# A two-stage kernel on one core: the first two chunks reordered, the softmax front one batch sooner, the sums in two tiles, the last batch step-major

## The chip, the core and the metric

The kernel runs on one core of one Trainium2 chip. The time is that of one execution on the device, in microseconds, from the first instruction to the last write of the output. Several executions are timed, and one more is taken by the hardware profiler. Five engines work side by side and wait for each other through semaphores: TensorE (PE, with PEld for its weight loads), VectorE (DVE), ScalarE (ACT), GpSimd (POOL) and SyncE (SP), which here issues all DMAs. Each engine takes its instructions in the order in which the program wrote them.

## The reference

A dynamic convolution over 7 taps with weights from a softmax, followed by a feed-forward layer with a squared ReLU. `x` is 8 x 4096 x 192 (32768 tokens), the weights of the convolution are one row of 7 for each token and each of 8 heads, and the matrices `w_in` (192 x 2048) and `w_out` (2048 x 192) come as float64.

```python
w = exp(weight_gen - max(weight_gen, -1))
w = w / (sum(w, -1) + 1e-09)
out = einsum('bshk,bskhg->bshg', w, x_unf)   # x_unf: the 7 tokens up to each, by head
h = out.reshape(B * S, D) @ w_in
g = maximum(h, 0) ** 2
return g @ w_out
```

## The kernel before

The 32768 tokens are cut into 64 chunks of 512 (four tiles of 128 tokens, `TC`). A chunk passes three stages: the convolution (`conv_steps`, on DVE, exponential on ACT), which leaves 192 x 512 numbers with the features on the partitions; the first matmul (`mm1`) with `w_in`, 2048 features in 8 groups `j` of 256; ReLU and square on ACT; and the second matmul (`mm2`) with `w_out` into the sums `acc` in PSUM, one tile of four banks.

From chunk 1 on both matmuls work in float16 pairs: a number is a high part and a low part. `xh`/`xl` are those of x, `gh`/`gl` those of g, `W` holds two parts of `w_in`, `V` three columns of `w_out` (hi, lo, and hi shifted down, "sh"). Chunk 0 is computed in float32, since the scales of the pairs are not known yet: the float64 weights are decoded meanwhile (`dec(u, step)`: unit u of 8, four of `w_in` and four of `w_out`, steps 0 on ACT, 1 on POOL (unit 0: DVE), 2 to 4 on DVE, 5 the largest magnitude), and then converted (`cvt[u]`: hi on ACT, lo on DVE, and sh on ACT for `w_out`).

The main loop at L581 runs over chunks c and batches b = 0 to 3, two groups j each. In a batch the program writes: `mm1` of both groups; `gl` of the batch before ("late"); at b = 1 the end of the chunk before (`finish`: `tmp` on ACT and `o_sb` on DVE for each half of acc, then `store`); at b = 3 the split of the next chunk's x; `mm2` of the batch before; then ACT's six activations (relu, square, relu, high, square, high), and last what stands in the table `todo` for this (c, b). `plan_conv(m)` deals the steps of chunk m's convolution onto that table. The first matmul of a batch fills two tiles `ph`, of which there are two, so relu must have read one before the next group can use it.

The convolution ends in a turn from tokens to features. Chunks below `N_PE` turn on PE by matmuls with the identity (L328), into the two `ph` tiles; the others by a DVE transpose of 32 x 32 blocks and a DMA to DRAM (`xd`) and back (`xT`). The split reads `xT` or `ph`: a cast on ACT (`xh`), then a subtract on DVE (`xl`).

The steps of one convolution, in order: maximum, subtract, exponential (ACT), sum, reciprocal, norm, seven products (mul) with six sums (add) between them, turn. Inputs come in groups of two chunks (`load_group`), with a scale for each group (`size_steps`: `total` on ACT, `scales` on DVE).

Of the kernel before, what the change touches and what calls it, by code (L numbers as in the profile page):

```python
# [25 lines left out]
def kernel(  # L26
# [366 lines left out]

    def mm2_first(fb):
        if fb == 0:
            accs[0] = ps_o.tile([P, TC, N], F32, name="acc")
        j, i = divmod(fb, 2)
        v = wfull[NU + j // 2][:, j % 2, i * D:(i + 1) * D]
        for t in range(TC):
            o = accs[0][:, t, 0:D]  # L400
            nc.tensor.matmul(o, rgs[0, j][:, i, t * P:(t + 1) * P], v, start=fb == 0, stop=fb == NF - 1)  # L401

    def mm2(c, b):
        if b == 0:
            accs[c] = ps_o.tile([P, TC, N], F32, name="acc")
        acc = accs[c]
        for t in range(TC):
            for j in (2 * b, 2 * b + 1):
                for i in range(2):
                    fb = 2 * j + i  # L410
                    first, last = fb == 0, fb == NF - 1
                    two = [(ghs[c, j], 0, 2 * D, 0), (gls[c, j], 0, D, 2 * D)]
                    if last:
                        two.reverse()
                    for n, (g, c0, c1, v0) in enumerate(two):
                        nc.tensor.matmul(  # L416
                            acc[:, t, c0:c1], g[:, i, t * P:(t + 1) * P], V[:, fb, v0:v0 + c1 - c0],
                            start=first and n == 0, stop=last and n == 1,
                        )
        for j in (2 * b, 2 * b + 1):  # L420
# [17 lines left out]
    def store(c):  # L438
        nc.sync.dma_start(out=out_v[:, c * TC:(c + 1) * TC, :], in_=outs.pop(c))
# [217 lines left out]
```

## Time and profile before

| | us |
|---|---|
| three runs, median (lowest to highest) | 2166.41 (2163.73 to 2166.71) |
| profiled execution | 2165.77 |
| its span, first to last instruction | 2164.0 |
| busy: PE, DVE, ACT, POOL | 2099.1, 1735.5, 1760.0, 9.1 |
| mean granted clock of PE | 0.995 |

The profile lists instructions with their start, duration and tiles; in square brackets the idle time of the engine before it and what ended that. Busy PE is near its whole span, but matmuls overlap in the records, so the distances between starts say more than busy time. "L416" is a line of the kernel before.

### The profile page before, as it was taken

What the parts mean: (1) busy time and instruction counts of PE and PEld (TensorE: products, weight loads), DVE (VectorE), ACT (ScalarE), POOL (GpSimd) and SP (SyncE); (2) the same over time, 40 slices, a digit from 0 to 9 for tenths busy, and PEclk for the clock granted to TensorE, in tenths of its full rate; (3) what the DMA queues carried; (4) which work ended last, traced back from release to release, by engine and by line L of the source; (5) the groups of instructions that cost most, each with busy time, mean ns of one, the idle gap of its engine ahead of it and who ended that gap; (6) DMA issues with size and microseconds to landing.
All of it is one profiled execution on the core that took longest, in us unless ns stands there. A gap on an engine that the chain in (4) does not pass through costs nothing.

```text
span 2164.0 us, 41491 instructions
## 1 busy us (share of the span) xinstructions
PE 2099.1 (97%) x17652; PEld 1182.8 (55%) x17652; DVE 1735.5 (80%) x2302; ACT 1760.0 (81%) x2006; POOL 9.1 (0%) x14
## 2 busy tenths in 40 slices
PE   7789999999999999999999999999999999999998
PEld 5555555555555555555555555555555555555555
DVE  7668878878878878878878878878878878778773
ACT  5667888888888888888888888888888888888886
POOL 1000000000000000000000000000000000000000
PEclk9999999999999999999999999999999999999999
DMA  6111222231222221222221232231232231232220
GB/s 176 38 38 47 73 89 78 71 89 44 75 89 74 76 89 38 81 89 69 80 89 38 82 89 67 82 89 38 82 89 67 82 89 37 83 89 66 54 60 15
DMA packets 99466, 156.26 MB, mean 72 GB/s; under 512 B 8281, under 2 KB 63705, under 8 KB 95313
## 3 DMA queue, kind: packets, MB, share of 16 engines
q1 hardware_dynamic: 99280, 153.61, 24.0%
q8 instruction: 138, 2.26, 0.4%
q14 instruction: 48, 0.39, 0.1%
HBM read 104.82 MB, written 48.76 MB: 71 GB/s over the span
## 4 chain that ended last, share of the span: by engine, by line
PE 78%; DVE 10%; ACT 9%; issue 2%; DMA 0%; SPq 0%; ACTq 0%
PE acc L416 40%; PE ph L373 36%; DVE gl L392 6%; ACT g L384 3%; ACT g L380 3%; ACT gh L388 1%; PE acc L401 1%; ACT tmp L435 1%; DVE o_sb L436 1%; DVE sm L264 1%; DVE sm L263 1%; ACT wt L262 1%; DVE pr L281 0%; PE ph L328 0%; DVE pr L276 0%
## 5 line engine op out<-in xcount | busy, mean ns | idle before, releaser
L416 PE MATMUL acc<-V,gh 128*128 128x384 f16 x4032 | 1024.1, 328 | 19.1 <-DVE o_sb L436 12.7
L416 PE MATMUL acc<-V,gl 128*128 128x192 f16 x4032 | 950.4, 247 | 16.1 <-DVE gl L392 16.1
L373 PE MATMUL ph<-xh,W 64*128 64x512 f16 x6048 | 778.9, 377 | 3.7 <-DVE xl L310 3.7
L373 PEld LDWEIGHTS <-W 64*128 64x128 f16 x9072 | 422.0, 94 | 540.4 <-issue 63.0
L380 ACT ACTIVATE g<-ph 128x1024 f32<-128x1024 f32 x504 | 510.3, 1013 | 209.8 <-PE ph L373 209.8
L392 DVE SCALAR_TENSOR_TENSOR gl<-gh,g 128x1024 f16<-128x1024 f16 x504 | 591.9, 1214 | 37.0 <-ACT gh L388 37.0
L416 PEld LDWEIGHTS <-gh 128*128 128x128 f16 x4032 | 392.0, 98 | 335.6 <-issue 84.2
L384 ACT ACTIVATE g<-g 128x1024 f32<-128x1024 f32 x512 | 538.2, 1052 | 8.0
L388 ACT ACTIVATE gh<-g 128x1024 f16<-128x1024 f32 x504 | 530.1, 1052 | 8.0
L416 PEld LDWEIGHTS <-gl 128*128 128x128 f16 x4032 | 395.1, 98 | 64.6 <-DVE gl L392 35.9
L276 DVE TENSOR_TENSOR pr<-xt,wt 128x768 f32<-128x768 f32 x448 | 416.2, 952 | 1.3 <-DMA xt<-in_x_dram 1.2
L373 PE MATMUL ph<-xl,W 64*128 64x512 f16 x3024 | 408.8, 376 | 0.0
L281 DVE TENSOR_TENSOR pr<-pr 128x768 f32<-128x768 f32 x382 | 363.7, 952 | 2.3
L263 DVE TENSOR_REDUCE sm<-wt 128x32 f32<-128x224 f32 x64 | 24.7, 386 | 285.1 <-ACT wt L262 285.1
L435 ACT ACTIVATE tmp<-acc,f 128x384 f32<-128x384 f32 x126 | 73.1, 580 | 123.6 <-DVE o_sb L436 117.9
L436 DVE SCALAR_TENSOR_TENSOR o_sb<-acc,f,tmp 128x384 f32<-128x384 f32 x126 | 77.4, 614 | 45.0 <-ACT tmp L435 45.0
L310 DVE TENSOR_TENSOR xl<-xT,xh 128x512 f16<-128x512 f32 x180 | 113.3, 684 | 0.0
L309 ACT CAST xh<-xT 128x512 f16<-128x512 f32 x180 | 98.5, 610 | 0.0
L344 DVE STREAM_TRANSPOSE xr<-pr 128x768 f32<-128x768 f32 x60 | 58.7, 978 | 2.1
L134 ACT ACTIVATE junk<-xt 128x1536 bf16<-128x1536 f32 (+1 forms) x32 | 47.3, 1477 | 0.0
L328 PE MATMUL ph<-ident,pr 128*64 128x128 f32 x288 | 20.3, 309 | 17.4 <-DVE pr L281 14.5
L257 DVE SCALAR_TENSOR_TENSOR wt<-wt,up,sm 128x224 f32<-128x224 f32 x63 | 28.5, 452 | 2.2
(59 smaller groups left out, 325.9 us busy)
## 6 DMA issues: line engine op xcount, KB each, us to landing
xT<-xd SPq DMA_DIRECT2D x120, 384.0 KB, 4.9
xt<-in_x_dram SPq DMA_DIRECT2D x31, 1344.0 KB, 8.7
out_dram<-o_sb SPq DMA_DIRECT2D x64, 384.0 KB, 5.5
xd<-xr SPq DMA_DIRECT2D x240, 96.0 KB, 2.1
wt<-in_weight_gen_dram SPq DMA_DIRECT2D x31, 224.0 KB, 5.4
raw<-in_moe_w_in_dram SPq DMA_DIRECT2D x16, 192.0 KB, 5.5
raw<-in_moe_w_out_dram SPq DMA_DIRECT2D x4, 768.0 KB, 4.4
xt<-in_x_dram SPq DMA_DIRECT2D x2, 384.0 KB, 4.9
```

What stands on the lines that cost most here:

```text
L276: tt(out=dst, in0=src, in1=wk.broadcast_to([P, n, G]), op=ALU.mult)
L281: tt(out=prs[k0], in0=prs[k0], in1=prs.pop(k), op=ALU.add)
L309: nc.scalar.copy(xh, xs)
L310: tt(out=xl, in0=xs, in1=xh, op=ALU.subtract)
L373: nc.tensor.matmul(ph[:, i], w[rows, k * P:(k + 1) * P], xx[rows, k], **fl)
L380: act(r, phs.pop((c, j)), AF.Relu, scale=RHO * LIFT ** 0.5)
L384: act(r, r, AF.Square)
L388: act(gh, rgs[c, j], AF.Copy, scale=1.0 / LIFT)
L392: stt(out=gl, in0=ghs[c, j], scalar=-LIFT, in1=rgs.pop((c, j)), op0=ALU.mult, op1=ALU.add)
L416: nc.tensor.matmul(acc[:, t, c0:c1], g[:, i, t * P:(t + 1) * P], V[:, fb, v0:v0 + c1 - c0], start=first and n == 0, stop=last and n == 1,)
L435: act(tmp, acc[:, :, D:2 * D], AF.Copy, scale=f)
L436: stt(out=o, in0=acc[:, :, 0:D], scalar=f, in1=tmp, op0=ALU.mult, op1=ALU.add)
```

## The change

It has four parts.

First two chunks. The maximum, subtract and exponential of chunk 1 move into the convolution of chunk 0; for that the second half of the first group's weights is loaded ahead of the halo rows. The decoding of a unit is spread differently, unit 0's step 1 goes to POOL like the others, the copies of chunk 0's turned x come ahead of unit 2's decode, and the scale of group 0 is computed before chunk 0's first matmul. `w_out` is converted before chunk 1 instead of inside it, but for the lo parts of units 5 to 7. The convolution of chunk 2 starts before chunk 1: eight of its steps (up to two products) there, and three steps in each batch of chunk 1. `N_PE` is 3, so chunk 3 turns by DMA.

Softmax front. For later chunks, maximum, subtract and exponential of chunk m stand at (m-2, 0); the rest begins at (m-2, 1) with the sum. Chunks 3 and 4 have places of their own.

Sums. `acc` is two tiles of two banks, one for each half that `finish` reads.

Last batch. The very last `mm2` runs its two groups j one after the other over all four tiles, and each half of the last chunk is stored by itself.

```diff
-    N_PE = 4
+    N_PE = 3
...
         nc.sync.dma_start(out=xt[:, HALO:HALO + TC, :], in_=x_v[:, 0:TC, :])
+        nc.sync.dma_start(out=wf[:, TC:, :], in_=wg_v[:, TC:TG, :])
...
-        eng = nc.gpsimd if u > 0 else nc.vector
+        eng = nc.gpsimd
...
+    def new_accs(c):
+        accs[c] = [ps_o.tile([P, 2, N], F32, name=f"acc{i}") for i in range(2)]
...
+        order = [(t, j) for t in range(TC) for j in (j0, j1)]
+        if c == NCH - 1 and b == NB - 1:
+            order = [(t, j) for j in (j0, j1) for t in range(TC)]
+        for t, j in order:
+            acc = accs[c][t // 2][:, t % 2]
...
-        acc = accs[c][:, 2 * p:2 * p + 2]
+        acc = accs[c][p]
...
+    conv1, split1 = conv_steps(1, 1)
+    for f in sts[:7]:
+        f()
+    for f in conv1[:3]:
+        f()
+    dec(0, 0, 1)
+    for f in sts[7:]:
+        f()
+    dec(1, 0, 1)
+    dec(0, 2, 3, 4)
     for f in sp:
         f()
-    dec(0, 1, 2, 3, 4)
-    conv1, split1 = conv_steps(1, 1)
     total, scales = size_steps(0)
+    total()
+    dec(2, 0, 1)
...
+    conv2[2]()
+    cvt[NU][0]()
+    cvt[NU][2]()
     cvt[0][1]()
     for f in split1:
         f()
+    fit_back()
     cvt[1][1]()
+    cvt[NU][1]()
+    for u in range(1, NU):
+        cvt[NU + u][0]()
+        cvt[NU + u][2]()
+    scales()
     descale(0)
+    descale(1)
+    for f in conv2[3:8]:
+        f()
...
+        a, splits[m] = conv_steps(m, 0)
+        b = 3 if m == N_PE else 2 if m == N_PE + 1 else 0
+        for f in a[:3]:
+            at(m - 2, b, f)
         if m == N_PE:
-            spread(a, m - 2, 3, (0.3, 0.7, 1))
+            spread(a[3:], m - 1, 0, (0.4, 0.75, 1))
+        elif m == N_PE + 1:
+            spread(a[3:], m - 2, 3, (0.25, 0.65, 1))
         else:
-            spread(a, m - 2, 1, (0.3, 0.55, 0.75, 1))
-        splits[m] = p
+            spread(a[3:], m - 2, 1, (0.25, 0.55, 0.73, 1))
...
-    for u in range(NU):
-        if u > 1:
-            at(1, u - 2, cvt[u][1])
-        for f in cvt[NU + u]:
-            at(1, u, f)
+    for u in range(2, NU):
+        at(1, u - 2, cvt[u][1])
+    for u in range(1, NU):
+        at(1, u - 1, cvt[NU + u][1])
+    spread(conv2[8:], 1, 0, (0.25, 0.5, 0.75, 1))
...
                 for p in range(2):
                     finish(c - 1, p)
-                store(c - 1)
+                    if c == NCH:
+                        store(c - 1, p, p + 1)
+                if c < NCH:
+                    store(c - 1)
```

Three places in the order of instructions show what the diff only implies. The first is ACT in a steady chunk, from the last activations of batch 0 on: the activations g and gh, the exponential (wt), and the two `tmp` of the chunk that ends. Before:

```order
L384 ACTIVATE g<-g 128x1024
L388 ACTIVATE gh<-g 128x1024
L435 ACTIVATE tmp<-acc,f 128x384 x2
L380 ACTIVATE g<-ph 128x1024
L384 ACTIVATE g<-g 128x1024
L380 ACTIVATE g<-ph 128x1024
L388 ACTIVATE gh<-g 128x1024
L384 ACTIVATE g<-g 128x1024
L388 ACTIVATE gh<-g 128x1024
L262 ACTIVATE wt<-wt 128x224
```

And now (its line numbers are those of the changed kernel, one to six lines off):

```order
L383 ACTIVATE g<-g 128x1024
L387 ACTIVATE gh<-g 128x1024
L261 ACTIVATE wt<-wt 128x224
L440 ACTIVATE tmp<-acc_3138,f 128x384
L440 ACTIVATE tmp<-acc_3139,f 128x384
L379 ACTIVATE g<-ph 128x1024
L383 ACTIVATE g<-g 128x1024
```

The exponential moved from the end of batch 1 to the end of batch 0, ahead of the `tmp` pair, and the pair reads two tiles. DVE at the same place, from the transpose of the next chunk on, before:

```order
L344 STREAM_TRANSPOSE xr<-pr 128x4x6x32
L392 SCALAR_TENSOR_TENSOR gl<-gh,g 128x1024 x2
L436 SCALAR_TENSOR_TENSOR o_sb<-acc,f,tmp 128x384 x2
L260 TENSOR_REDUCE mx<-wt 128x32
L261 TENSOR_TENSOR wt<-wt,mx 128x224
L263 TENSOR_REDUCE sm<-wt 128x32
L264 TENSOR_SCALAR sm<-sm 128x32
L264 RECIPROCAL sm<-sm 128x32
L257 SCALAR_TENSOR_TENSOR wt<-wt,up,sm 128x224
L392 SCALAR_TENSOR_TENSOR gl<-gh,g 128x1024 x2
```

And now:

```order
L343 STREAM_TRANSPOSE xr<-pr 128x4x6x32
L259 TENSOR_REDUCE mx<-wt 128x32
L260 TENSOR_TENSOR wt<-wt,mx 128x224
L391 SCALAR_TENSOR_TENSOR gl<-gh,g 128x1024 x2
L441 SCALAR_TENSOR_TENSOR o_sb<-acc_2741,f,tmp 128x384
L441 SCALAR_TENSOR_TENSOR o_sb<-acc_2742,f,tmp 128x384
L262 TENSOR_REDUCE sm<-wt 128x32
L263 TENSOR_SCALAR sm<-sm 128x32
L263 RECIPROCAL sm<-sm 128x32
L256 SCALAR_TENSOR_TENSOR wt<-wt,up,sm 128x224
L275 TENSOR_TENSOR pr<-xt,wt 128x768
L391 SCALAR_TENSOR_TENSOR gl<-gh,g 128x1024 x2
```

Between subtract and sum there now stand two `gl` and two `o_sb`, and one product stands behind the norm. The second place is ACT around the first batch of chunk 1, from the split of x (before) or the last conversions (now) to the copy of chunk 0's result (`o_sb`). Before:

```order
L309 CAST xh<-ph 128x512 x3
L380 ACTIVATE g<-ph 128x1024
L384 ACTIVATE g<-g 128x1024
L380 ACTIVATE g<-ph 128x1024
L388 ACTIVATE gh<-g 128x1024
L384 ACTIVATE g<-g 128x1024
L388 ACTIVATE gh<-g 128x1024
L232 ACTIVATE V<-du,fit 128x4x192
L236 ACTIVATE V<-V 128x4x192
L134 ACTIVATE junk,a<-xt 128x1536
L262 ACTIVATE wt<-wt 128x224
L431 COPY o_sb<-acc 128x384 x2
```

And now:

```order
L231 ACTIVATE V<-du,fit 128x4x192
L235 ACTIVATE V<-V 128x4x192
L231 ACTIVATE V<-du,fit 128x4x192
L235 ACTIVATE V<-V 128x4x192
L379 ACTIVATE g<-ph 128x1024
L383 ACTIVATE g<-g 128x1024
L379 ACTIVATE g<-ph 128x1024
L387 ACTIVATE gh<-g 128x1024
L383 ACTIVATE g<-g 128x1024
L387 ACTIVATE gh<-g 128x1024
L436 COPY o_sb<-acc_435 128x384
L436 COPY o_sb<-acc_436 128x384
```

The conversion, the total and the exponential that stood between the activations and the copy are gone from there. The third place is DVE where chunk 3's convolution ends (sums, then the turn), before, with the split from PE's tile:

```order
L276 TENSOR_TENSOR pr<-xt,wt 128x768
L281 TENSOR_TENSOR pr<-pr 128x768 x2
L310 TENSOR_TENSOR xl<-ph,xh 128x512 x3
L260 TENSOR_REDUCE mx<-wt 128x32
L261 TENSOR_TENSOR wt<-wt,mx 128x224
```

And now, with the DVE transpose, whose result goes through DRAM to `xT`:

```order
L275 TENSOR_TENSOR pr<-xt,wt 128x768
L280 TENSOR_TENSOR pr<-pr 128x768 x2
L343 STREAM_TRANSPOSE xr<-pr 128x4x6x32
L259 TENSOR_REDUCE mx<-wt 128x32
L260 TENSOR_TENSOR wt<-wt,mx 128x224
L391 SCALAR_TENSOR_TENSOR gl<-gh,g 128x1024 x2
L309 TENSOR_TENSOR xl<-xT,xh 128x4x4x32 x3
```

The split of chunk 3 stands one pair of `gl` behind the transpose.

More of the change, by code (lines that the diff above doesn't have):

```diff
@@ L404, in mm2 @@
         if b == 0:
[L405 to L420, printed above, removed]
+            new_accs(c)
+        j0, j1 = 2 * b, 2 * b + 1
+        order = [(t, j) for t in range(TC) for j in (j0, j1)]
[3 more added lines that the diff above has]
+            acc = accs[c][t // 2][:, t % 2]
+            for i in range(2):
+                fb = 2 * j + i
+                first, last = fb == 0, fb == NF - 1
+                two = [(ghs[c, j], 0, 2 * D, 0), (gls[c, j], 0, D, 2 * D)]
+                if last:
+                    two.reverse()
+                for n, (g, c0, c1, v0) in enumerate(two):
+                    nc.tensor.matmul(
+                        acc[:, c0:c1], g[:, i, t * P:(t + 1) * P], V[:, fb, v0:v0 + c1 - c0],
+                        start=first and n == 0, stop=last and n == 1,
+                    )
+        for j in (j0, j1):
             del ghs[c, j], gls[c, j]
@@ L475 @@
     relu(0, 1)
-    total()
     relu(0, 2)
-    dec(2, 2, 3, 4)
-    dec(1, 5)
     dec(4, 0, 1)
+    dec(3, 2, 3, 4)
+    dec(2, 5)
+    dec(3, 5)
+    mm1(0, 4)
+    mm1(0, 5)
     square(0, 0)
     relu(0, 3)
-    mm1(0, 4)
-    mm1(0, 5)
-    dec(3, 2, 3, 4)
     square(0, 1)
-    dec(2, 5)
-    dec(3, 5)
     relu(0, 4)
+    dec(5, 0, 1)
     mm1(0, 6)
-    fit_matmul(0, ps_o, "acc", [P, TC, N])
+    fit_matmul(0, ps_o, "acc0")
     mm1(0, 7)
-    dec(5, 0, 1)
-    for f in conv1[:2]:
-        f()
-    relu(0, 5)
-    conv1[2]()
-    scales()
+    for f in conv1[6:8]:
+        f()
     dec(4, 2, 3, 4)
     square(0, 2)
+    relu(0, 5)
     square(0, 3)
+    dec(6, 0, 1)
     relu(0, 6)
-    for f in conv1[3:6]:
-        f()
     fit_scales(0)
-    dec(6, 0, 1)
     relu(0, 7)
@@ L509 @@
     load_group(1)
+    for f in conv1[8:10]:
+        f()
     dec(5, 2, 3, 4)
@@ L514 @@
     cvt = {u: convert_steps(u) for u in range(2 * NU)}
-    for f in conv1[6:10]:
+    for f in conv1[10:12]:
         f()
@@ L521 @@
     cvt[1][0]()
-    for f in conv1[10:13]:
+    for f in conv1[12:14]:
         f()
@@ L525 @@
     dec(7, 5)
-    for u in range(2, NU):
-        cvt[u][0]()
-    for f in conv1[13:15]:
+    cvt[2][0]()
+    cvt[3][0]()
+    for f in conv1[14:16]:
         f()
-    for fb in range(NF - 3):
+    for fb in range(NF - 4):
         mm2_first(fb)
-    fit_matmul(1, ps_h, "ph", [P, 2, N])
-    for f in conv1[15:17]:
+    fit_matmul(1, ps_h, "ph")
+    total, scales = size_steps(1)
+    total()
+    conv2, split2 = conv_steps(2, 1)
+    for f in conv1[16:18]:
         f()
     fit_scales(1)
-    for f in conv1[17:]:
+    conv2[0]()
+    conv2[1]()
+    for f in conv1[18:]:
         f()
-    for fb in range(NF - 3, NF):
+    for fb in range(NF - 4, NF):
         mm2_first(fb)
-    fit_back()
+    conv2[2]()
+    cvt[NU][0]()
+    cvt[NU][2]()
     cvt[0][1]()
```

52 lines of the change are left out of this document (20 added, 32 removed).

## The prediction

> **What bounds the kernel now.** I read the busy time by stage first, cut at the first matmul of chunk 1 (72.81), of chunk 4 (201.69) and of the last batch (2145.20). Columns: the stage, its length, then PE, PEld, DVE, ACT and POOL busy, granted clock, DMA share.
>
> ```profile
> 0.00:72.81 72.81, 57.45 (x421) 43.49 (x422) 57.61 (x87) 35.94 (x48) 9.07 (x14) 0.98 0.51 153
> 72.81:201.69 128.88, 105.70 (x881) 61.02 (x881) 92.52 (x128) 90.14 (x105) 0.00 (x0) 0.93 0.10 32
> 201.69:2145.20 1943.51, 1923.79 (x16254) 1070.97 (x16254) 1580.50 (x2083) 1626.67 (x1846) 0.00 (x0) 1.00 0.25 72
> 2145.20:2164.00 18.80, 12.18 (x101) 7.29 (x100) 4.91 (x5) 7.25 (x9) 0.00 (x0) 0.91 0.05 22
> ```
>
> In the long stage PE is busy for 1923.79 of 1943.51: only what stops PE counts there. In chunks 1 to 3 it lacks 23 us. So I next want the length of a batch that nothing disturbs, and what stops PE elsewhere: the starts of two batches, three apart, near the end; two stops in one steady pair of chunks; and the totals of waits for those (waiter, releaser, us in total, times, longest).
>
> ```profile
> 2121.15 0.82 PE L373 MATMUL ph<-xh,W 64*128 64x512 f16 x6
> 2145.20 0.82 PE L373 MATMUL ph<-xh,W 64*128 64x512 f16 x6
> 994.52 0.32 PE L416 MATMUL acc<-V,gh 128*128 128x384 f16 x1 [0.32 <-DVE o_sb L436]
> 1003.73 0.26 PE L416 MATMUL acc<-V,gl 128*128 128x192 f16 x1 [0.38 <-DVE gl L392]
> DVE sm L263 <- ACT wt L262: 285.1, 62, 4.8
> PE acc L416 <- DVE gl L392: 16.1, 34, 2.3
> PE acc L416 <- DVE o_sb L436: 12.7, 29, 3.7
> ```
>
> An undisturbed batch is 24.05 / 3 = 8.017 us. From 201.69 to 2145.20 there are 59 chunks and 3 batches, 239 batches: 1916.1 at that pace, 1943.5 measured, so **27.4 us** are lost, some 0.9 per pair of chunks. The two stops (0.32 and 0.38) come once per pair; the rest is their restart. The engines behind them, around the same place:
>
> ```profile
> 986.51 0.95 DVE L276 TENSOR_TENSOR pr<-xt,wt 128x768 f32<-128x768 f32 x1
> 987.38 1.94 DVE L281 TENSOR_TENSOR pr<-pr 128x768 f32<-128x768 f32 x2
> 989.36 0.98 DVE L344 STREAM_TRANSPOSE xr<-pr 128x768 f32<-128x768 f32 x1
> 993.14 0.58 ACT L435 ACTIVATE tmp<-acc,f 128x384 f32<-128x384 f32 x1 [2.32 <-DVE o_sb L436]
> 993.76 0.62 DVE L436 SCALAR_TENSOR_TENSOR o_sb<-acc,f,tmp 128x384 f32<-128x384 f32 x1 [0.65 <-ACT tmp L435]
> 994.70 0.39 DVE L261 TENSOR_TENSOR wt<-wt,mx 128x224 f32<-128x224 f32 x1
> 999.92 0.39 DVE L263 TENSOR_REDUCE sm<-wt 128x32 f32<-128x224 f32 x1 [4.83 <-ACT wt L262]
> 1001.32 2.35 DVE L392 SCALAR_TENSOR_TENSOR gl<-gh,g 128x1024 f16<-128x1024 f16 x2
> ```
>
> DVE stands still for 4.83 us because the exponential (wt L262) lies in ACT's queue behind six activations of the batch; the next two gl start late, at 1001.32, and PE waits for the second. The other stop is one PSUM tile: PE may not start the next chunk's sums before the second o_sb, which waits for the second tmp, which waits for the first o_sb.
>
> **Steady stage: -27.4.** Subtract and exponential now stand one batch earlier and the sum one batch later, so the exponential has run when DVE asks for its sum. DVE work of the fullest batch (b = 0), start to start from the rows: two gl 2.27, a sum 0.87, product and two sums 2.85 (986.51 to 989.36), transpose 0.90, maximum and subtract 0.83: 7.72, below 8.017. The added wait is ACT's for that subtract; queued behind it are the two tmp and the next relu. The transpose ended at 990.3 in this batch, so the subtract would end at 991.1, the exponential at 991.5, both tmp (no longer tied to an o_sb) at 992.6, against 993.7 now. gl then ends at 993.4 and the first o_sb at 994.0, before PE asks at 994.2; the second sum is asked for 2 us later. Both stops go. Bounds: 0 and -27.4; I take the full sum since every step has at least 0.2 us to spare.
>
> **Start: -0.7.** PE works almost without a gap from 22.54 to 72.81.
>
> ```profile
> 20.61 0.91 ACT L180 ACTIVATE du<-raw 128x768 f32<-128x768 f32 x1 [4.09 <-DMA raw<-in_moe_w_in_dram]
> 21.42 1.55 ACT L299 COPY xT<-ph 128x512 f32<-128x512 f32 x3
> 21.60 1.15 POOL L181 TENSOR_SCALAR du<-du 128x768 f32<-128x768 f32 x1 [3.99 <-ACT du L180]
> 22.10 1.46 DVE L184 SCALAR_TENSOR_TENSOR du<-raw,du 128x768 uint32<-128x768 uint32 x1
> 65.94 2.84 PE L328 MATMUL ph<-ident,pr 128*64 128x128 f32 x48 [2.90 <-DVE back L219]
> 72.81 0.82 PE L373 MATMUL ph<-xh,W 64*128 64x512 f16 x6
> ```
>
> The copies of xT wait behind the decode of unit 2, which waits for its DMA until 20.61; now they stand ahead of it and start when PE's transposes end. That chain is later by the extra issue on SP ahead of the eight halo loads (0.5) and, for the step of unit 0 that moves from DVE to POOL, by a clash: 1.46 instead of 0.96 beside a POOL step. So 19.8 + 1.0, copies from 20.9, PE 1.1 later at 22.0: -0.5. The transposes of chunk 1 now follow one sum and two softmax steps instead of two sums: 0.2 less than the 2.90. Chunk 1 starts at 72.1.
>
> The clash has a rule. The Trainium skill ("SBUF — State Buffer", "Who interferes with whom") says that a VectorE instruction with two SBUF inputs and a reading GpSimd one exclude each other for a whole instruction. By it the two POOL steps in that chain could cost 2.3 instead of 0.5, and the sum would be 1.8 higher; the row shows 0.5.
>
> **Chunks 1 to 3: -20.5.** Rows first: PE's stops, a conversion on each engine, and the DMA turn of chunk 4, with its time to landing.
>
> ```profile
> 79.91 1.06 ACT L388 ACTIVATE gh<-g 128x1024 f16<-128x1024 f32 x1
> 80.87 0.92 ACT L232 ACTIVATE V<-du,fit 128x768 f16<-128x768 f32 x1
> 82.76 1.01 DVE L233 SCALAR_TENSOR_TENSOR W<-du,fit,W 128x768 f16<-128x768 f32 x1
> 87.09 0.48 PE L416 MATMUL acc<-V,gh 128*128 128x384 f16 x1 [6.34 <-ACT o_sb L431]
> 119.34 4.51 PE L328 MATMUL ph<-ident,pr 128*64 128x128 f32 x48 [4.74 <-DVE pr L281]
> 162.45 0.82 PE L373 MATMUL ph<-xh,W 64*128 64x512 f16 x6 [1.88 <-DVE xl L310]
> 179.07 0.48 PE L416 MATMUL acc<-V,gh 128*128 128x384 f16 x1 [3.67 <-DVE o_sb L436]
> 184.43 1.82 SPq L350 DMA_DIRECT2D xd<-xr  x4
> 188.00 1.24 SPq L355 DMA_DIRECT2D xT<-xd  x2
> DMA to landing us min/median/max: 3.9/4.9/7.4
> ```
>
> The walk, by batch (c,b):
> - (1,0) and (1,1): only first matmuls, 72.1 to 80.1. The four conversions that stood behind chunk 1's activations are on ACT before it (each with its shifted copy, some 1.8 on ACT); the first batch's activations end at 81.0 - 0.7 = 80.3, and the first o_sb copy (0.4) follows at once: 80.8, where PE now waits until 87. DVE has, after the split of x, two lo parts (0.95 each), small steps 1.5, softmax 1.5, two products, two lo parts and three taps, and gets to gl at 80.2: the second at 82.5. Then 3.5 us of sums: 86.0 (93.6 before).
> - (1,2), (1,3): no wait; 94.0 and 102.0. Then chunk 2's transposes, 2.84, and 1.88 for the split, as at 162.45: (2,0) at 106.7 (125.7 before). The 4.74 is gone since the convolution of chunk 2 ran as filler.
> - (2,0) to (2,2) at full pace, (2,3) at 130.8. DVE is full: from 106.6 it has 23.7 us until the transpose of chunk 3, which no longer goes through PE (4.7 less there).
> - The turn costs instead: 3.57 to the second issue, 0.6, 4.9: xT lands 9.1 after the transpose, 139.4. The split stands in ACT's queue ahead of relu of (2,3), so relu runs from 141.0; PE, ready at 138.8, gets a free ph at 142.1 and then the last gl at 148.4. (3,1) starts at 151.8.
> - (3,1): seven taps of chunk 4 and the subtract of chunk 5 stand ahead of gl on DVE, to 155.3; first o_sb at 158.3 where PE asks at 155.8: ends 162.3. (3,2): ten items more, gl to 169.1: ends 172.5. (3,3) free, (4,0) at **180.5** against 201.69.
>
> Bounds: 12 free batches (96.2) give -12.2 more; all 128.9 gives the 20.5 back. xT's landing of 3.9 to 7.4 alone is -1.0 to +2.5. Another cost is the clock: after 2.90 idle, 48 transposes took 2.84; after 4.74, 4.51; after 3.67 a matmul took 0.48. The new stop of 3.3 lies between them. The Trainium skill ("TensorE: Matmul & The Clock Gate", Part 1) puts the gate at an idle window of about 3.4 us that runs freely, so by it the stop may fall either way; half pace would take until 153 at most in (3,0), and the wait for o_sb until 158.3 swallows that. The row's 1.7 for 48 transposes bounds it where nothing swallows it.
>
> **End: -2.6.**
>
> ```profile
> 2153.39 1.22 DVE L392 SCALAR_TENSOR_TENSOR gl<-gh,g 128x1024 f16<-128x1024 f16 x1 [0.81 <-ACT gh L388]
> 2154.67 0.34 PE L416 MATMUL acc<-V,gl 128*128 128x192 f16 x2 [0.74 <-DVE gl L392]
> 2158.15 0.58 ACT L435 ACTIVATE tmp<-acc,f 128x384 f32<-128x384 f32 x1 [4.79 <-PE acc L416]
> 2160.03 0.62 DVE L436 SCALAR_TENSOR_TENSOR o_sb<-acc,f,tmp 128x384 f32<-128x384 f32 x1 [0.65 <-ACT tmp L435]
> 2160.68 0.33 SPq L439 DMA_DIRECT2D out_dram<-o_sb  x1
> ```
>
> Step-major, the step whose gl is ready fills the 0.74 and its restart, so sums end at 2157.2, not 2158.15; two tmp back to back save another 1.2: -2.2. The last store is half as large: 3.3 from issue to end now; bounds 0 and -1.2, I take -0.4.
>
> **Sum.** -27.4 - 0.7 - 20.5 - 2.6 = -51.2; span 2112.8. The profiled execution took 2165.77, 1.77 above its span: **2114.6**. It lies 0.64 below the median shown, too little to matter; 0.2%, about what can be told from no change, is 4.3 us.
>
> **Rivals.**
> - The exponential's wait takes the old one's place: if the subtract ends a few us into b = 1, tmp, relu and gl slip and PE still stops. For: DVE has 0.3 us free in b = 0. Against: 4.83 us per chunk come free. Half to none of the gain: 2128 to 2142. Chance 0.13.
> - Chunks 2 and 3 only trade PE's transposes for DMA and DVE waits (landing 7.4, cold clock, DVE behind for longer): half of 20.5 lost, 2125, up to 2136. Chance 0.15.
> - Slower: DVE falls behind for good. Exponential and both tmp (1.5) are over before relu's input, 2.2 us into the batch, if the subtract ends 0.6 into b = 1; from there the gl of that batch, which end 9.4 after its start in the walk and are asked for at 12.0, can slip by 2.6. So it decides from 3.2 us into b = 1, and each us beyond costs 60 chunks 1 us: at 4.4 us 60 x 1.2 = 72, 2187; from 0.9 beyond the point it passes the old time. DVE's 26.5 us of work in a chunk of 32 (1580.50 over 59.75 chunks) speaks against it. 0.03. Between, within 0.2%: 0.02.
> - The split does nothing (PE still waits for both o_sb): those end at 994.6 in the walk, 0.4 late, some 11 us; inside the first rival.
>
> The forecast has 0.67, by itself 2106 to 2126. The range takes in the free batches at one end and most of the first two rivals at the other: 2104 to 2134. Faster 0.95, same 0.02, slower 0.03.
>
> **What would show it.** Right: DVE's wait for the exponential gone from the list; steady batches all 8.02; chunk 1 at 72, (2,0) at 107, (4,0) at 180 with one stop near 139; o_sb's copy near 81. Wrong: ACT waiting for the subtract by more than 1 us per chunk, batches of 8.4 still there, or PE stops of over 4 us in chunks 2 and 3.

## The result and the profile after

| | before | after |
|---|---|---|
| median (lowest to highest), us | 2166.52 (2163.73 to 2166.71) | 2113.02 (2112.54 to 2114.16) |
| profiled execution, its span, us | 2165.77, 2164.0 | 2114.16, 2112.4 |
| busy PE, DVE, ACT, us | 2099.1, 1735.5, 1760.0 | 2081.8, 1763.9, 1756.0 |

The time after is 0.9757 of the time before, with a 95% interval of 0.974 to 0.9774, and the forecast was 2114.6. The window view of the kernel after, cut at the starts of the batches (1,0), (2,0), (4,0) and of the last one, has in each row the stretch, its length, busy time (and count) of PE, PEld, DVE, ACT and POOL, the granted clock of PE, and the DMA's share and rate:

```profile
0.00:71.55 71.55, 57.33 (x420) 44.32 (x421) 59.27 (x94) 43.20 (x58) 10.23 (x15) 0.98 0.52 156
71.55:105.91 34.36, 31.18 (x289) 17.85 (x289) 25.93 (x33) 28.86 (x33) 0.00 (x0) 1.00 0.03 12
105.91:179.95 74.04, 65.08 (x545) 36.48 (x545) 64.46 (x90) 53.66 (x62) 0.00 (x0) 1.00 0.22 66
179.95:2096.19 1916.24, 1916.24 (x16253) 1073.22 (x16252) 1609.37 (x2084) 1623.08 (x1847) 0.00 (x0) 1.00 0.25 73
2096.19:2112.40 16.21, 12.01 (x101) 7.39 (x100) 4.91 (x5) 7.25 (x9) 0.00 (x0) 1.00 0.06 24
```

From 179.95 on PE's busy time equals the stretch, to the hundredth: it does not stop in 239 batches, which take 8.02 us each. Set against the kernel before and the forecast's walk, stage by stage (us):

| stage | before | forecast | after |
|---|---|---|---|
| up to (1,0) | 72.81 | 72.1 | 71.55 |
| chunk 1, (1,0) to (2,0) | 52.85 | 34.6 | 34.36 |
| chunk 2 | 36.79 | 35.4 | 36.19 |
| chunk 3 | 39.24 | 38.4 | 37.85 |
| (4,0) to the last batch | 1943.51 | 1916.1 | 1916.24 |
| last batch and what follows | 18.80 | 16.2 | 16.21 |

Groups of the kernel after (line, engine, operation, output <- input, count, then busy time and mean ns, then idle time ahead and what ended it):

```profile
L262 DVE TENSOR_REDUCE sm<-wt 128x32 f32<-128x224 f32 x64 | 24.0, 375 | 0.5 <-ACT wt L261 0.5
L440 ACT ACTIVATE tmp<-acc,f 128x384 f32<-128x384 f32 x126 | 65.2, 567 | 3.3 <-PE acc L421 3.3
L421 PE MATMUL acc<-V,gh 128*128 128x384 f16 x4032 | 1015.9, 327 | 3.2 <-DVE o_sb L441 2.3 <-ACT o_sb L436 0.6 <-ACT gh L387 0.3
L421 PE MATMUL acc<-V,gl 128*128 128x192 f16 x4032 | 947.4, 246 | 3.2 <-DVE gl L391 3.2
```

DVE's wait for the exponential is down to 0.5 us in all, and no tmp waits for an o_sb any more; what idle time is left ahead of the second matmul lies in the first chunks. Most of the stops of PE there, with the transposes and the first matmul of chunks 2 and 3, from the timeline of the kernel after (the largest not shown is 0.92 for a gl, at 148.34):

```profile
61.85 4.38 PE L327 MATMUL ph<-ident,pr 128*64 128x128 f32 x48 [2.63 <-DVE pr L280]
80.13 0.32 PE L421 MATMUL acc<-V,gh 128*128 128x384 f16 x1 [0.64 <-ACT o_sb L436]
81.79 0.26 PE L421 MATMUL acc<-V,gl 128*128 128x192 f16 x1 [0.47 <-DVE gl L391]
101.19 2.84 PE L327 MATMUL ph<-ident,pr 128*64 128x128 f32 x48
105.91 0.82 PE L372 MATMUL ph<-xh,W 64*128 64x512 f16 x6 [1.88 <-DVE xl L309]
142.10 0.82 PE L372 MATMUL ph<-xh,W 64*128 64x512 f16 x6 [3.80 <-ACT g L379]
157.93 0.32 PE L421 MATMUL acc<-V,gh 128*128 128x384 f16 x1 [2.16 <-DVE o_sb L441]
167.42 0.26 PE L421 MATMUL acc<-V,gl 128*128 128x192 f16 x1 [1.15 <-DVE gl L391]
```

Most of the large stops of before (6.34 at o_sb, 4.74 ahead of chunk 2's transposes, 3.67 at o_sb) are gone; a new one of 3.80 has come at chunk 3's turn by DMA.

### The profile page after: what moved, and what is told of

It reads as the page before. It is cut to its first block, busy times and chain, and to the rows that moved or that the text cites. A ratio compares the mean times of both kernels' runs of the same rounds, so it can differ in the third digit from the quotient of the medians.

```text
span 2112.4 us, 41481 instructions
## 1 busy us (share of the span) xinstructions
PE 2081.8 (99%) x17604; PEld 1179.3 (56%) x17604; DVE 1763.9 (84%) x2302; ACT 1756.0 (83%) x2006; POOL 10.2 (0%) x15
## 4 chain that ended last, share of the span: by engine, by line
PE 95%; DVE 4%; ACT 1%; DMA 0%; SPq 0%; issue 0%; POOL 0%; DVEq 0%; ACTq 0%; POOLq 0%
PE ph L372 47%; PE acc L421 47%; DVE pr L275 1%; DVE pr L280 1%; PE acc L403 1%; DVE gl L391 1%; PE ph L327 0%; DMA xT<-xd 0%; ACT xh L308 0%; DVE xl L309 0%; DVE o_sb L441 0%; SPq L113 0%; DMA xt<-in_x_dram 0%; DMA xd<-xr 0%; ACT g L383 0%
## 5 line engine op out<-in xcount | busy, mean ns | idle before, releaser
L391 DVE SCALAR_TENSOR_TENSOR gl<-gh,g 128x1024 f16<-128x1024 f16 x504 | 613.4, 1223 | 275.2 <-ACT gh L387 270.2
L275 DVE TENSOR_TENSOR pr<-xt,wt 128x768 f32<-128x768 f32 x448 | 423.0, 956 | 2.9 <-DMA xt<-in_x_dram 0.7
L309 DVE TENSOR_TENSOR xl<-xT,xh 128x512 f16<-128x512 f32 x183 | 115.4, 685 | 28.3 <-ACT xh L308 28.3
L441 DVE SCALAR_TENSOR_TENSOR o_sb<-acc,f,tmp 128x384 f32<-128x384 f32 x126 | 71.7, 609 | 2.6 <-ACT tmp L440 2.6
L440 ACT ACTIVATE tmp<-acc,f 128x384 f32<-128x384 f32 x126 | 65.2, 567 | 3.3 <-PE acc L421 3.3
L261 ACT ACTIVATE wt<-wt 128x224 f32<-128x224 f32 x64 | 24.0, 375 | 10.9 <-DVE wt L260 10.9
```

The lines of the kernel that those rows point to most:

```text
L275: tt(out=dst, in0=src, in1=wk.broadcast_to([P, n, G]), op=ALU.mult)
L309: tt(out=xl, in0=xs, in1=xh, op=ALU.subtract)
L391: stt(out=gl, in0=ghs[c, j], scalar=-LIFT, in1=rgs.pop((c, j)), op0=ALU.mult, op1=ALU.add)
L440: act(tmp, acc[:, :, D:2 * D], AF.Copy, scale=f)
L441: stt(out=o, in0=acc[:, :, 0:D], scalar=f, in1=tmp, op0=ALU.mult, op1=ALU.add)
```

## The experiments

All are the changed kernel with one part undone or moved. Medians of four or five executions each; 2113.02 is the changed kernel's, and executions of one of these kernels lie up to 2.9 us apart (q6_both_late), so differences near 1 us settle nothing.

| run | edit | median, us | to the changed kernel |
|---|---|---|---|
| s1_late_two | softmax front late again, two tiles kept | 2112.64 | -0.4 |
| s2_early_one | sums in one tile again, early front kept | 2116.89 | +3.9 |
| s3_late_one | both undone | 2143.83 | +30.8 |
| q3_wout_late | w_out converted inside chunk 1 again | 2125.06 | +12.0 |
| q5_conv2_late | chunk 2's convolution inside chunk 1 again | 2111.80 | -1.2 |
| q6_both_late | both of these | 2127.73 | +14.7 |
| p1_chunk3_on_pe | chunk 3 turned on PE | 2113.13 | +0.1 |
| q4_tail_undone | last batch and store as before | 2114.97 | +2.0 |
| p2_chunk3_early | chunk 3's convolution in chunk 1 | 2104.71 | -8.3 |
| q1_turn_first | chunk 2's maximum behind chunk 1's sum | 2112.42 | -0.6 |
| best1 | p2 and q1 together | 2103.13 | -9.9 |

### The steady stops: which of the two edits removes them

The two edits, undone apart and together (`s3` has both pieces):

```diff
 # s1: the front of the later chunks goes back to batch 1
-        for f in a[:3]:
+        for f in a[:3] if m <= N_PE + 1 else []:
             at(m - 2, b, f)
...
-            spread(a[3:], m - 2, 1, (0.25, 0.55, 0.73, 1))
+            spread(a, m - 2, 1, (0.3, 0.55, 0.75, 1))
 # s2: one tile of four banks
-        accs[c] = [ps_o.tile([P, 2, N], F32, name=f"acc{i}") for i in range(2)]
+        acc = ps_o.tile([P, TC, N], F32, name="acc")
+        accs[c] = [acc[:, 2 * i:2 * i + 2] for i in range(2)]
...
```

> The changed kernel with the softmax front of the chunks from 5 on put back where it was (all steps in batch 1 of two chunks ahead, at 0.3, 0.55, 0.75 and 1 of the batch), the sums still in two tiles. Theory, that either part alone takes both steady stops away: with two tiles the scaled copy of the second half no longer waits for the first half's sum, ScalarE is about 1 us ahead, the exponential comes about 1.2 us earlier and the late gl ends about 1 us before TensorE asks for it; so the steady stretch from (4,0) to the last batch stays within 2 us of the 1916.2 us of the changed kernel and the time is 2113 to 2115, although VectorE waits for the exponential again (some 280 us idle ahead of the sum in all). Rival, that the two stops add (0.38 and 0.32 us per pair of chunks times about 31 to 40 pairs): the stop at gl comes back, +12 to +15 us, 2125 to 2128. Rival, that the softmax's place does it all: +27 us, 2140.

> The changed kernel with the sums of one chunk back in one tile of four blocks, the softmax front still one batch sooner. Theory, that either part alone takes both steady stops away: the second sum ends at about 992.9 in the chunk in which the changed kernel's TensorE asks for its tile at 993.7, so TensorE doesn't wait: within 2 us of the changed kernel, 2113 to 2115. Rival, that the stops add: the one at the sums comes back, +10 to +13 us, 2123 to 2126. Rival, that the two tiles do it all: +27 us, 2140.

> Both parts put back in the changed kernel: the softmax front of the chunks from 5 on late, the sums in one tile; the start, the first three chunks and the end stay as changed. The forecast's term for the steady stretch says +27 us: 2138 to 2142, the stretch from (4,0) to the last batch 1916.2 + 27 = 1943 us. Rival, that part of the 27 us came from elsewhere (the place of chunk 3's convolution, the first chunks' order): less than +20 us.

Measured from (4,0) to the last batch: s1 177.22 to 2093.47, 1916.25 us; s2 179.87 to 2096.11, 1916.24; s3 180.29 to 2124.87, 1944.58. So each edit alone takes away all of it, and only with both undone do 28.3 us come back. The timeline of s3 where it stops:

```profile
972.08 0.61 DVE L442 SCALAR_TENSOR_TENSOR o_sb<-acc,f,tmp 128x384 f32<-128x384 f32 x1
972.72 0.58 ACT L441 ACTIVATE tmp<-acc,f 128x384 f32<-128x384 f32 x1 [2.33 <-DVE o_sb L442]
973.20 1.01 ACT L379 ACTIVATE g<-ph 128x1024 f32<-128x1024 f32 x1
974.10 0.32 PE L422 MATMUL acc<-V,gh 128*128 128x384 f16 x1 [0.33 <-DVE o_sb L442]
979.10 0.37 ACT L261 ACTIVATE wt<-wt 128x224 f32<-128x224 f32 x1
979.51 0.39 DVE L262 TENSOR_REDUCE sm<-wt 128x32 f32<-128x224 f32 x1 [4.83 <-ACT wt L261]
980.90 2.35 DVE L391 SCALAR_TENSOR_TENSOR gl<-gh,g 128x1024 f16<-128x1024 f16 x2
983.31 0.26 PE L422 MATMUL acc<-V,gl 128*128 128x192 f16 x1 [0.38 <-DVE gl L391]
```

It reads as one chain through both stops: the second tmp waits 2.33 us for the first o_sb, so relu starts at 973.20, 3.49 us after its batch (969.71), and ACT, not PE, sets its time; the exponential stands six activations behind it, at 979.10; DVE waits 4.83 us for that, and both gl are late. In s1 (batch start 987.02) the link through the tile is gone:

```profile
987.07 1.03 ACT L440 ACTIVATE tmp<-acc,f 128x384 f32<-128x384 f32 x2
989.18 1.02 ACT L379 ACTIVATE g<-ph 128x1024 f32<-128x1024 f32 x1 [1.08 <-PE ph L372]
995.49 0.39 DVE L262 TENSOR_REDUCE sm<-wt 128x32 f32<-128x224 f32 x1 [5.30 <-ACT wt L261]
996.89 2.35 DVE L391 SCALAR_TENSOR_TENSOR gl<-gh,g 128x1024 f16<-128x1024 f16 x2
```

and the group of that sum over the whole run of s1:

```profile
L262 DVE TENSOR_REDUCE sm<-wt 128x32 f32<-128x224 f32 x64 | 24.7, 386 | 288.7 <-ACT wt L261 288.7
```

Relu starts 2.16 us into the batch, 1.33 sooner, and now waits for PE. DVE stands idle for the exponential longer than ever, 5.30 us here and 288.7 us in all, but the two gl end 12.22 us into the batch and not 13.54 as in s3: in time, and PE does not stop. **The largest idle time of DVE in the list of groups cost nothing by itself.** In the changed kernel it is not gone either, it has moved: there DVE stands 270.2 us ahead of its gl, waiting for gh on ACT. In s2 the tile still ties tmp to o_sb, and the chain is cut at its other end:

```profile
991.63 0.58 ACT L441 ACTIVATE tmp<-acc,f 128x384 f32<-128x384 f32 x1 [1.07 <-DVE o_sb L442]
992.24 0.62 DVE L442 SCALAR_TENSOR_TENSOR o_sb<-acc,f,tmp 128x384 f32<-128x384 f32 x1 [0.65 <-ACT tmp L441]
```

The second o_sb ends at 992.86, 3.20 us into its batch; in s3 it ended 4.25 in, 0.2 after PE asked. What s2 loses (3.9 us by the medians, 1.3 between the profiled executions, 2115.43 and 2114.16) lies elsewhere. From the last batch to the end it takes 17.5 us in place of 16.2, since there the second tmp waits for the first o_sb as before. From (1,0) to (4,0) it takes 110.08 us in place of 108.40, but the granted clock in that stretch was 0.97 against 1.00, which is some 3.3 us, so that this part is not shown to be a price of the one tile.

### Chunk 1: the conversion of w_out, and chunk 2's convolution

```diff
 # q3: all of w_out's conversion in chunk 1's batches, unit u in batch u
-    cvt[NU][0]()
-    cvt[NU][2]()
     cvt[0][1]()
...
-    cvt[NU][1]()
-    for u in range(1, NU):
-        cvt[NU + u][0]()
-        cvt[NU + u][2]()
     scales()
...
-    for u in range(1, NU):
-        at(1, u - 1, cvt[NU + u][1])
+    for u in range(NU):
+        for f in cvt[NU + u]:
+            at(1, u, f)
 # q5: chunk 2's front and first products in chunk 1 too
-    conv2[0]()
-    conv2[1]()
...
-    conv2[2]()
...
-    for f in conv2[3:8]:
-        f()
...
-    spread(conv2[8:], 1, 0, (0.25, 0.5, 0.75, 1))
+    spread(conv2, 1, 0, (0.15, 0.4, 0.7, 1))
```

> The changed kernel with the conversion of w_out (16-bit halves of V, for the second matmul from chunk 1 on) put back into chunk 1's four batches, all else as changed. Theory, that the early conversion is what ended the stop of TensorE in (1,1): a stop of 2 to 4 us at the first second-layer matmul of chunk 1 comes back (79.6 to 80.1 is its place in the changed kernel, where 0.64 and 0.47 us are left), (4,0) starts 2 to 4 us later than 179.95 and the time is 2115 to 2117. Rival, that VectorE's and ScalarE's surplus in (1,3) (7.4 us of VectorE idle there) takes the conversion back in: within 1 us of the changed kernel, 2112 to 2114. Rival, that work put back ahead of chunk 2's turn delays that as well: +5 us or more.

> The changed kernel with chunk 2's softmax front and first convolution steps taken out of the stretch before chunk 1's first batch and spread over chunk 1's four batches as they were before the change; the conversion of w_out stays early. Theory, that the early conversion alone makes the room (VectorE idles 7.4 us ahead of chunk 2's split in the changed kernel, and the moved steps are 6.1 us of VectorE work): the transposes of chunk 2 wait less than 1 us, (2,0) starts within 1.5 us of 105.9, 2112 to 2115. Rival, by the forecast's step (the 4.74 us stop ahead of chunk 2's transposes is gone because its convolution ran as filler): the stop comes back, with its slow transposes, +5 to +7 us, 2118 to 2120.

> Both parts of chunk 1's new order put back in the changed kernel: w_out converted in chunk 1's batches and chunk 2's softmax and convolution spread over them. From (1,0) to (2,0) the kernel before took 52.85 us, the changed one 34.36, the one with only w_out late 45.32, the one with only chunk 2's convolution late 34.53. Theory, that w_out's conversion is what fills chunk 1 and the convolution costs only where the conversion stands beside it: 50 to 53 us, the stop ahead of chunk 2's transposes back at 4 to 5 us, the time 2129 to 2132. Rival, that the parts add: 45.3 + 0.2, 2125. Rival, that the rest of the new order (chunk 2's size and scales ahead of chunk 1, two tiles for the sums) carries part of it: 47 to 49 us, 2127.

From (1,0) to (2,0), all on the changed kernel's other parts (us):

| | convolution of chunk 2 early | inside chunk 1 |
|---|---|---|
| w_out early | 34.36 | 34.53 |
| w_out inside chunk 1 | 45.32 | 49.68 |

q3 lost 12.0 us where its first theory said 2 to 4; only its last rival, 5 or more, allowed for that. Its timeline shows where:

```profile
80.61 1.02 DVE L232 SCALAR_TENSOR_TENSOR V<-du,fit,V 128x768 f16<-128x768 f32 x1 [5.57 <-ACT V L231]
85.42 0.34 PE L421 MATMUL acc<-V,gl 128*128 128x192 f16 x1 [3.23 <-DVE gl L391]
100.13 1.02 DVE L232 SCALAR_TENSOR_TENSOR V<-du,fit,V 128x768 f16<-128x768 f32 x1 [5.28 <-ACT V L231]
```

Each lo part on DVE waits for its hi part on ACT, and that stands behind the six activations of the batch, so DVE waits 5.57, 1.53, 5.28 and 3.16 us in the four batches and the gl behind it are late: the same shape of wait as that for the exponential. The conversion is a ping-pong between two full queues, and its price is the waits and what they bring on, not its work. For what they bring on is in part PE's clock: the same 289 or 290 matmuls of this stage kept PE busy for 31.18 us in the changed kernel and 30.90 in q5 (granted clock 1.00 in both), but for 34.89 in q3 (0.89), 35.05 in q6 (0.93) and 35.74 in the kernel before (0.90). So some 4 of the 11 to 15 us are slower matmuls, and the rest is PE standing still. q5's theory held, but for (1,0), which came 2.3 us sooner there: with w_out early the place of chunk 2's convolution does not matter, since DVE then has time free ahead of chunk 2's split; in the changed kernel's timeline:

```profile
103.82 0.69 DVE L309 TENSOR_TENSOR xl<-ph,xh 128x512 f16<-128x512 f32 x1 [7.38 <-ACT xh L308]
```

The stop ahead of chunk 2's transposes stays small with either of the two edits undone by itself, first q5, then q3:

```profile
99.10 2.84 PE L327 MATMUL ph<-ident,pr 128*64 128x128 f32 x48 [0.85 <-DVE pr L280]
112.20 2.84 PE L327 MATMUL ph<-ident,pr 128*64 128x128 f32 x48 [1.04 <-DVE pr L280]
```

Only in q6, with both undone, are the stop and the slow transposes of before back:

```profile
80.71 0.32 PE L421 MATMUL acc<-V,gh 128*128 128x384 f16 x1 [3.66 <-ACT o_sb L436]
112.41 4.51 PE L327 MATMUL ph<-ident,pr 128*64 128x128 f32 x48 [4.39 <-DVE pr L280]
```

Of the 18.5 us that chunk 1 gained, 15.1 are w_out's conversion while chunk 2's convolution is late (11.0 while it is early), the convolution's place is worth 0.2 with w_out early and 4.4 with it late, and the remaining 3.2 (52.85 to 49.68) belong to the rest. The first theory for q6 gave 50 to 53 us, its last rival 47 to 49; it came between them.

### Chunk 3

```diff
 # p1: turned on PE, as before
+        a, p = conv_steps(m, int(m == 3))
+        if m == 3:
+            for f in a[:3]:
+                at(1, 3, f)
+            spread(a[3:], 2, 0, (0.25, 0.5, 0.75, 1))
+            for f in p:
+                at(2, 3, f)
+            return
 # p2: by DMA, two batches sooner; chunk 4 then one batch sooner
+    conv3, splits[3] = conv_steps(3, 0)
+    for f in conv3[:3]:
+        at(1, 2, f)
+    for f in conv3[3:10]:
+        at(1, 3, f)
...
+    spread(conv3[10:], 2, 0, (0.5, 1))
...
-            spread(a[3:], m - 2, 3, (0.25, 0.65, 1))
+            spread(a[3:], m - 2, 2, (0.35, 0.65, 1))
```

> The changed kernel with chunk 3 turned by TensorE's 96 half-word transposes at the end of chunk 2, as before, and not by DMA: its convolution starts after chunk 1's last batch and is spread over (2,0). Theory, that chunk 3's way costs as much by DMA as by TensorE and the first chunks were won by the order alone: the start of (4,0) stays within 2 us of 179.95 (from (2,3) to (4,0) 48 to 52 us, as 49.7 in the changed kernel), the time 2111 to 2115. Rival, that the DMA turn is itself the gain (9 us of TensorE for the transposes and their copies): +5 to +9 us, 2118 to 2122. Rival, that the DMA turn was a loss that the rest covered: -3 to -6 us, 2107 to 2110.

> The changed kernel with chunk 3's convolution moved forward into the 7.4 us for which VectorE stands idle in (1,3), its softmax front in (1,2), and its turn by DMA so two batches sooner; chunk 4's then in (2,2) to (3,0). Theory, that the 3.8 us stop at chunk 3's DMA turn (142.10) and the stops behind it (2.16 at 157.9, 1.15 and 0.47 at 167.4) come from VectorE having chunk 3's whole convolution in (2,0) to (2,2): from (2,3) to (4,0) 40 to 45 us in place of 49.7, (4,0) 5 to 9 us sooner, 2104 to 2108. Rival, that VectorE's work only moves and (1,3) to (2,2) grow by as much: within 2 us, 2111 to 2115. Rival, that the earlier convolution delays chunk 2's turn, so that (2,0) starts later than 105.9 by more than 3 us and the time is longer, 2116 or more.

p1: from (2,3) at 129.82 to (4,0) at 179.43, 49.61 us, against 49.74 by DMA. The turn by DMA was neither a gain nor a loss (the rival that priced PE's way at 9 us had it too dear: 2.84 for the 48 transposes and a wait of 1.88 behind them, 4.7). p2: from 129.86 to 170.57, 40.71 us. Its rows show chunk 3's first batch start without a stop and chunk 2's turn unharmed:

```profile
103.72 0.69 DVE L309 TENSOR_TENSOR xl<-ph,xh 128x512 f16<-128x512 f32 x1 [1.99 <-ACT xh L308]
105.81 0.82 PE L372 MATMUL ph<-xh,W 64*128 64x512 f16 x6 [1.88 <-DVE xl L309]
137.88 0.82 PE L372 MATMUL ph<-xh,W 64*128 64x512 f16 x6
150.53 0.32 PE L421 MATMUL acc<-V,gh 128*128 128x384 f16 x1 [0.57 <-DVE o_sb L441]
```

DVE's 7.38 idle us ahead of the split became 1.99, and the stops of 3.80, 2.16 and 1.15 are replaced by one of 0.57.

### The end

```diff
-        if c == NCH - 1 and b == NB - 1:
-            order = [(t, j) for j in (j0, j1) for t in range(TC)]
...
-                    if c == NCH:
-                        store(c - 1, p, p + 1)
-                if c < NCH:
-                    store(c - 1)
+                store(c - 1)
```

> The changed kernel with its end undone: the last batch's second-layer matmuls in the old order (block by block, not step by step) and the last chunk stored whole, the sums still in two tiles. Theory by the forecast's terms: the first half's sum starts sooner than with the step order, but the last two matmul steps end behind the late gl; from the last batch's start to the end 16.2 us become 18.4 to 18.8 us, 2115 to 2116. Rival, that the block order costs nothing with two tiles and only the half store counts: +0.4 us, 2113 to 2114.

Last batch (2093.82) to the end (2111.4): 17.6 us, against 16.2 changed and 18.8 before. The expectation missed, by taking the forecast's whole term for the step order and the half store; the 1.2 in it for the two tmp hangs on the two tiles, which q4 keeps. The rival, 0.4, missed as well. The timelines, first q4 and then the kernel after (last batch at 2096.19):

```profile
2104.82 0.58 ACT L438 ACTIVATE tmp<-acc,f 128x384 f32<-128x384 f32 x1 [2.83 <-PE acc L419]
2106.78 0.58 ACT L438 ACTIVATE tmp<-acc,f 128x384 f32<-128x384 f32 x1 [1.38 <-PE acc L419]
```

```profile
2107.26 0.58 ACT L440 ACTIVATE tmp<-acc,f 128x384 f32<-128x384 f32 x1 [2.90 <-PE acc L421]
2108.24 0.58 ACT L440 ACTIVATE tmp<-acc,f 128x384 f32<-128x384 f32 x1 [0.40 <-PE acc L421]
```

With two tiles and the old order, the first half is read while PE still works on the second, so only one tmp and one o_sb remain behind the last matmul: that is 1.2 of the 2.6. The step order brings the last tmp from 12.96 to 12.05 us into the batch, and with the half store that is the other 1.4.

### A version that beats both

```diff
-    conv2[0]()
-    conv2[1]()
     for f in conv1[18:]:
         f()
+    conv2[0]()
+    conv2[1]()
```

> The changed kernel with chunk 2's maximum and subtract (VectorE, 0.83 us) put behind chunk 1's last sum and not ahead of it. Theory: the 2.63 us for which TensorE waits for that sum before chunk 1's 48 transposes become 1.8, and the time 0.8 us shorter. If the half pace of these transposes (4.38 us for 48 in the changed kernel, 2.84 where the clock is whole) hangs on the length of the idle time, they too become 2.84: 2.4 us in all, 2110 to 2111. Rival, that the pace doesn't hang on it: 0.8 us, 2112 to 2113.

> Both shifts together: chunk 3's convolution in VectorE's idle time of (1,3) and its turn two batches sooner (2104.7 alone), and chunk 2's maximum and subtract behind chunk 1's last sum (2112.4 alone, against 2113.0). Theory, that the two lie in different stages and add: 0.6 to 0.8 us less than the first alone, 2103.5 to 2104.3. Rival, that the second is given back at the softmax of chunk 2 or at gl in (1,1), as its own trace hints (the stop at gl in (1,1) grew from 0.2 to 0.79): 2104.5 to 2105.

q1 alone came out 0.6 us below, inside the spread of the changed kernel's runs, so by itself it settles little; three of its four executions lie at 2112.4. Its profiled one, the longest (2114.01), shows the wait ahead of chunk 1's transposes shortened, these at full pace, and a loss elsewhere. A row of its timeline, then one of its windows:

```profile
61.10 2.84 PE L327 MATMUL ph<-ident,pr 128*64 128x128 f32 x48 [1.91 <-DVE pr L280]
```

```profile
77.85:85.14 7.29, 6.03 (x32) 3.52 (x32) 7.29 (x8) 6.17 (x7) 0.00 (x0) 0.77 0.13 54
```

The clock granted there was 0.77, which costs 0.23 x 7.29 = 1.7 us; in best1 the same stretch, 77.74 to 83.36, takes 5.62 at full clock. There (1,0) starts at 69.17 and (4,0) at 168.70. best1 takes 2103.13 us, 0.971 of the time before (0.9697 to 0.9724), and is the fastest of all: p2's 8.3 us and 1.6 more. That is beyond both theories' figures (0.6 to 0.8, and at most 0.2), but the two intervals overlap (p2: 0.9701 to 0.9733), so that the last step is a gain is likely and not shown.

## Why the prediction was right, point by point

**Steady stage: right in size, too strict in its cause.** 27.4 us were forecast and 27.3 measured, and both stops went. The steps that failed are smaller. In its walk "gl then ends at 993.4 and the first o_sb at 994.0"; in the same chunk, with batch starts 0.40 apart, they ran much sooner:

```profile
989.80 0.37 ACT L261 ACTIVATE wt<-wt 128x224 f32<-128x224 f32 x1
989.93 1.23 DVE L391 SCALAR_TENSOR_TENSOR gl<-gh,g 128x1024 f16<-128x1024 f16 x1 [0.36 <-ACT gh L387]
990.08 1.03 ACT L440 ACTIVATE tmp<-acc,f 128x384 f32<-128x384 f32 x2
991.07 1.14 DVE L441 SCALAR_TENSOR_TENSOR o_sb<-acc,f,tmp 128x384 f32<-128x384 f32 x2
```

Both gl end by 991.2 and both o_sb by 992.2. The walk had started from the old trace's transpose at 990.3, which was itself late; once the stops are gone, that delay isn't there to begin with. The same flaw spoils the rival "the split does nothing", priced at some 11 us: s2 has one tile and loses none in this stage. So the exponential's place and the tile were two links of one chain, and the forecast, which used both, could not see that either was enough.

**Start: -1.3 where -0.7 was said**, right by two misses that cancel. The first matmul started at 21.71, not 22.0, though there were two clashes with POOL and not one. The timeline of the kernel after, the pairs of products beside the POOL steps:

```profile
12.53 0.83 POOL L180 TENSOR_SCALAR du<-du 128x768 f32<-128x768 f32 x1 [10.23 <-ACT du L179]
12.57 2.46 DVE L275 TENSOR_TENSOR pr<-xt,wt 128x768 f32<-128x768 f32 x2
15.68 1.03 POOL L180 TENSOR_SCALAR du<-du 128x768 f32<-128x768 f32 x1 [2.32 <-ACT du L179]
15.95 1.58 DVE L275 TENSOR_TENSOR pr<-xt,wt 128x768 f32<-128x768 f32 x1
```

A pair without POOL beside it takes 1.82 and a single product 0.95, so the clashes cost 0.64 and 0.63: 1.3 in all, more than the 0.5 taken. By the rule that the prediction weighed (the Trainium skill, "SBUF — State Buffer", "Who interferes with whom") DVE would stand until the POOL step beside it ends, which by these rows is 0.79 and 0.76, 1.55 in all; the measured 1.3 is somewhat less. The larger misses are the clock's. Windows of the kernel before and of the one after:

```profile
22.54:40.00 17.46, 17.46 (x74) 7.88 (x76) 13.02 (x20) 11.37 (x13) 2.77 (x4) 0.90 0.79 269
```

```profile
59.22:71.55 12.33, 9.70 (x80) 9.34 (x81) 7.99 (x21) 7.40 (x11) 0.00 (x0) 0.86 0.27 106
```

Before, the first matmuls after the 2.71 us stop ran at 0.90, 0.10 x 17.46 = 1.7 us lost; that stop is gone (0.30 is left of it). After, chunk 1's 48 transposes ran at half pace (4.38 us for 2.84) behind a stop of 2.63 which was shorter than the 2.90 of before: 0.14 x 12.33 = 1.7 lost there. The prediction named neither. Left are 0.83 from the first matmul and 0.27 from the shorter stop.

**Chunks 1 to 3: -20.5, as forecast, with half a reason in it.** (2,0) came at 105.91 for 106.7, (3,0) at 142.10 for 142.1, (4,0) at 179.95 for 180.5; chunk 2 took 0.8 us more than forecast and chunk 3 0.6 less, so in part the sum is right by luck. "The 4.74 is gone since the convolution of chunk 2 ran as filler" is the step that does not hold as it stands. q5 takes the filler out and the stop is 0.85; q3 leaves the filler and puts w_out's conversion back, and it is 1.04; only q6, without either, has it at 4.39. As in the steady stage, one of the two was enough, and the filler was not needed. What the stage gained, it gained mostly by w_out's early conversion (11.0 us by q3, against 0.2 for the convolution's place by q5), which the walk had as conversions that are on ACT before chunk 1. Of chunk 1's 18.5 us, 4.6 are faster matmuls (PE busy for 35.74 us before, 31.18 after); the walk took them in by going at full pace, without naming them.

The turn by DMA had its price right, a stop of 3.80 for 3.3, and it costs what PE's transposes cost (p1). The forecast said that the wait for o_sb would swallow a slow clock behind this stop. The changed kernel had none there; q1 had one, and took 37.86 us from (3,0) to (4,0) against 37.85, so it was swallowed. Half of the second rival's thought, that chunk 3 only trades PE's transposes for waits, is what happened, but chunk 2's and chunk 3's trades were never where the gain lay.

**End: -2.6, as forecast, and in its parts too.** The step order and the half store gave 1.4 (the forecast had 0.95 and 0.4). The two tiles gave 1.2, which the forecast had under two tmp back to back: with two tiles the second no longer waits for the first o_sb.

**The other rivals.** The exponential's wait did not take the old one's place (0.5 us of waiting in all), and DVE did not fall behind: in the steady stage it is busy 1609.37 of 1916.24 us.

## What to carry to other kernels

Before pricing two stops apart, follow each wait back across engines: if they are links of one chain, one cut takes them all, and the sum of two fixes is worth no more than either. A walk that starts from a late row of the old trace inherits the delay that the change removes; start it from the batch instead. The dearest thing in the crowded stretch here was not work but a ping-pong between two in-order queues (w_out's conversion, 11 to 15 us for 4 units, some 4 of them as a lower clock of PE), and idle time that lies ahead of a turn is the place for the next chunk's work (8.3 us).

## What the runs showed of the hardware that was not expected

PE's clock after a stop did not follow the stop's length, and differed from run to run of the same order. Behind 2.63 us idle at one place, the 48 transposes took 4.38, 4.41, 4.38, 4.20 and 4.18 us in the changed kernel, q3, p2, p1 and s3, and 2.84 in s1, s2 and q4; behind 1.91 us (q1, best1, q5, q6) always 2.84. Chunk 3's stop by DMA, 3.06 to 3.84 us, left the clock whole in two profiled runs (3.80 in the changed kernel, 3.63 in q4) and went with a clock of 0.50 in seven. In s3, q1, q5 and q6 the first six matmuls were already slow, 1.46 for 0.82; in s1, s2 and q3 they took 0.82 and the clock fell 0.9 to 1.3 us after PE had started again. In q1 PE was slow from 80.43 to 83.72 with nothing ahead of it but stops of 0.64, 0.79 and 0.47.

What does agree is how long a slow piece lasts. In the windows of these runs between 8 and 205 us the granted clock is 1.00 or 0.50, and each piece at 0.50 loses 1.71 us or twice that, so it lasts 3.4 us or 6.8. Two pieces of 6.8 are in the kernel before, 85.3 to 92.2 about its stop of 6.34 and 177.5 to 184.4 about the one of 3.67. The Trainium skill ("TensorE: Matmul & The Clock Gate", Part 1) has a gate that looks at windows of about 3.4 us; a window that starts anywhere would explain that like stops fare differently, but not a slow clock after 2.63 us, which is shorter than such a window. What sets it off is left open. A difference of 1.7 us, one such piece, between two runs of this kernel says nothing of an edit.
